# ScalarE's instruction order written out by hand from step 4 of a fused attention and feed-forward kernel

## The chip, the cores and the metric

One core of one Trainium2 chip runs the whole program. The metric is device time in microseconds, the median of several executions. Before the change it is 610.69 us (3 runs, 610.4 to 610.88).

## The reference

Attention with 4 batches, 8 heads, 768 positions and head dimension 64, in fp32. A query sees the first 8 keys and the 96 keys up to its own position, with a bias that grows with the distance. The output, as 3072 tokens by 512, is the input `x` of a gated feed-forward without a nonlinearity:

```
scores = where(keep, q @ k.T / 8 + bias, -1e9)
a = exp(scores - max(scores)); a = a / (sum(a) + 1e-9)
x = (a @ v), heads side by side        # 3072 x 512
out = ((x @ w1) * (x @ w2)) @ w3 @ w_out   # 512 -> 1024 -> 1024 -> 512
```

## The kernel before

**Attention.** The work is cut into 12 chunks of 256 queries (`c`, three to a batch) and 4 pairs of heads; a step `s` does two pairs of one chunk, so there are 24 steps (0 to 23) and a closing visit. In a step TensorE first does the products with the values of the step before (`values`, L457 and L459, into PSUM tile `v`), then the scores of this step (L406, into `s`). ScalarE and VectorE copy `v` out as a high and a low part (`xh`, `xl`, L63 and L64). Then `rows` does for each of 8 blocks (two pairs, two halves `j` of 128 queries, two heads `u`): VectorE adds the bias and takes the maximum (L421), ScalarE takes the exponential in place in `pr` and its sum (L422). `softmax` adds 1e-9 to the sums and inverts them on VectorE (L427, L428) and scales `pr`: the blocks of head `u` = 0 on ScalarE (L434, four a step, called the scalings here), the others on VectorE (L436). `flip` (called through `turn`, four times a step) transposes one half's blocks on TensorE (L445, L447) into the only buffer of `t`, and ScalarE copies it out as `ph` (L449). The first chunk of each batch (`c` = 0, 3, 6, 9) has narrower blocks, 128 columns for 232, in its first half.

**Feed-forward.** `FeedForward.run` is a generator of matmul pieces. For each of 8 blocks `f0` of the hidden dimension, TensorE computes `x @ w1` into a PSUM tile (`m_c_f0_0`, 12 matmuls, L161 to L163), which ScalarE evicts to `a` (L168); then `x @ w2` into the second tile (`m_c_f0_1`), which VectorE multiplies with `a` to `g` (L171); ScalarE and VectorE split `g` to `gh` and `gl` (L63, L64). There are two PSUM buffers for `m`, so `m` of the next block's first half takes the buffer that `a` has read. Then the product with the output weights (`w3 @ w_out`, folded into one matrix in the first steps) goes through tiles `o` (L178 to L180), ScalarE evicts them (L184) and SyncE stores them. From chunk 2 on a run does 512 tokens (two chunks), before that 256 with two blocks `f0` in one tile. The generator yields after 6 matmuls (a half tile), after the eviction, and after the split; `slices(k)` pulls `k` such pieces. A run of 512 tokens takes 48 pieces, the work of four steps: steps 8, 9, 10 and 11 have the run of chunks 2 and 3, and so on. Three of the four steps begin with a first half `m_c_f0_0` (f0 = 0, 3, 6), the fourth with a piece of `o`. Before step 4 there are weights to be prepared as well.

**What sets the order.** TensorE's instructions are in program order (L606). Those of VectorE and SyncE are in program order until the first steps are done, and are placed by the Tile scheduler afterwards (L607 to L620); those of ScalarE are placed by the scheduler throughout. In program order a step is: `visit`, `rows`, `softmax`, `loads` of the next step, then (from step 8 on) `slices(5)`, a `turn`, `slices(2)`, a `turn`, and so on. Each engine takes its own list in order and waits on semaphores of the others.

Of the kernel before, what the change touches and what calls it, by code (L numbers as in the profile page):

```python
# [22 lines left out]
NQ = 2  # L23
# [12 lines left out]
STEP = 2  # L36
# [24 lines left out]
def split(nc, hi, lo, x):  # L61

    nc.scalar.activation(hi, x, AF.Copy)  # L63
    nc.vector.tensor_tensor(out=lo, in0=x, in1=hi.bitcast(F32), op=ALU.subtract)  # L64


class FeedForward:
# [25 lines left out]
    def next(self, ring, slots):  # L93
        self.turn[ring] += 1
        return slots[(self.turn[ring] - 1) % len(slots)]
# [93 lines left out]
@with_exitstack  # L189
def attention_moe(ctx: ExitStack, tc: tile.TileContext, qk, vx, w1, w2, w3t, w_out, ns, out):  # L190
    nc = tc.nc
    cp = ctx.enter_context(tc.tile_pool(name="const", bufs=1))

    ident = cp.tile([P, P], F32, name="ident")
    make_identity(nc, ident)
    nt = cp.tile([P, 4], I32, name="nt")
    nf = cp.tile([P, 4], F32, name="nf")
    ff = FeedForward(ctx, tc, w1, w2, w3t, w_out, out)
    oki = cp.tile([P, 1], I32, name="oki")
    banded(tc, ff, ns, nt, nf, oki, ident, qk, vx)  # L200
    ok = nc.values_load(oki[0:1, 0:1])
    with tc.If(ok == 0):
        dense(tc, ff, nf, ident, qk, vx)
# [121 lines left out]
def banded(ctx, tc, ff, ns, nt, nf, oki, ident, qk, vx):  # L325


    nc = tc.nc
# [51 lines left out]
    def load(c, hp):  # L380
        b, cb = divmod(c, NCB)
        k0 = 0 if cb else BW
        qr = ld.tile([P, QW], F32, tag="qr", name=f"qr_{c}_{hp}")
        nc.sync.dma_start(out=qr[:, k0:], in_=qk[b, cb, hp, :, k0:])
        return qr

    def load_values(c, hp):
        b, cb = divmod(c, NCB)
        nw = 2 * NQ if cb else 2 * NQ - 1
        vr = ld.tile([P, 2 * NQ, 2 * D], F32, tag="vr", bufs=2 * STEP, name=f"vr_{c}_{hp}")  # L390
        nc.sync.dma_start(out=vr[:, :nw], in_=vx[b, cb, hp, :, :nw])
        return vr

    def scores(c, hp, qr):

        ps = sc[hp % STEP]
        for j in range(NQ):
            w0 = BW if c % NCB == 0 and j == 0 else 0  # L400
            for g in range(P // HQ):
                cols = slice(max(w0, g * HQ), BW + (g + 1) * HQ)
                q0 = KW + j * P + g * HQ
                for u in range(2):
                    m = qr[u * D:(u + 1) * D]
                    nc.tensor.matmul(ps[u][g * HQ:(g + 1) * HQ, j, cols], lhsT=m[:, q0:q0 + HQ], rhs=m[:, j * SLOT:][:, cols], start=True, stop=True)  # L406
        return ps

    def rows(c, hp, ps):

        pr = at.tile([P, NQ, 2, UW], F32, tag="pr", name=f"pr_{c}_{hp}")
        mx = at.tile([P, NQ, 2], F32, tag="mx", bufs=3, name=f"mx_{c}_{hp}")
        sm = at.tile([P, NQ, 2], F32, tag="sm", bufs=3, name=f"sm_{c}_{hp}")
        for j in range(NQ):
            first = c % NCB == 0 and j == 0
            w0 = BW if first else 0
            for u in range(2):
                h = 2 * hp + u
                bias = bias0[:, h, :] if first else biasw[:, h, :]
                m = mx[:, j, u:u + 1]  # L420
                nc.vector.tensor_tensor_reduce(out=pr[:, j, u, w0:], in0=ps[u][:, j, w0:UW], in1=bias, scale=-SCALE, scalar=3.0e38, op0=ALU.add, op1=ALU.min, accum_out=m)  # L421
                nc.scalar.activation(pr[:, j, u, w0:], pr[:, j, u, w0:], AF.Exp, bias=m, scale=-1.0, accum_out=sm[:, j, u:u + 1])  # L422
        return pr, sm

    def softmax(c, hp, pr, sm, scaled):

        nc.vector.tensor_scalar(out=sm, in0=sm, scalar1=1e-9, scalar2=None, op0=ALU.add)  # L427
        nc.vector.reciprocal(out=sm, in_=sm)  # L428
        for j in range(NQ):
            w0 = BW if c % NCB == 0 and j == 0 else 0  # L430
            for u in range(2):
                x, r = pr[:, j, u, w0:], sm[:, j, u:u + 1]
                if u == 0 or scaled is nc.scalar:
                    nc.scalar.activation(x, x, AF.Copy, scale=r)  # L434
                else:
                    nc.vector.tensor_scalar(out=x, in0=x, scalar1=r, scalar2=None, op0=ALU.mult)  # L436
        return pr

    def flip(c, hp, j, pr):

        first = c % NCB == 0 and j == 0
        nk = 1 if first else 2
        pt = ps_t.tile([P, 2, 2, P], F32, tag="t", name=f"t_{c}_{hp}_{j}")
        for u in range(2):
            nc.tensor.transpose(pt[:, u, 0], pr[:, j, u, BW:UW], ident)  # L445
            if not first:
                nc.tensor.transpose(pt[:, u, 1], pr[:, j, u, 0:P], ident)  # L447
        ph = at.tile([P, 2, 2, P], F32, tag="ph", bufs=4, name=f"ph_{c}_{hp}_{j}")
        nc.scalar.activation(ph[:, :, :nk], pt[:, :, :nk], AF.Copy)  # L449
        return ph  # L450

    def values(uu, c, hp, vr, phs):
        for j, ph in enumerate(phs):
            first = c % NCB == 0 and j == 0
            for u in range(2):
                rows, o = slice(u * D, (u + 1) * D), uu[u * D:(u + 1) * D, j * P:(j + 1) * P]
                nc.tensor.matmul(o, lhsT=vr[:, j, rows], rhs=ph[:, u, 0], start=True, stop=first)  # L457
                if not first:
                    nc.tensor.matmul(o, lhsT=vr[:BW, 2 * NQ - 1 - j, rows], rhs=ph[:BW, u, 1], start=False, stop=True)  # L459
# [3 lines left out]
    n = NC * NP // STEP  # L463
    pairs = lambda s: [divmod(STEP * s + i, NP) for i in range(STEP)]
# [3 lines left out]
    def slices(k):  # L468
        while k > 0 and work:
            if next(work[0], "end") == "end":  # L470
                work.pop(0)
            else:
                k -= 1

    def loads(s, keys=True, vals=True):
        if s < n and keys:
            qrs[s] = [load(*p) for p in pairs(s)]
        if s < n and vals:
            vrs[s] = [load_values(*p) for p in pairs(s)]

    def visit(s):
        if s:
            c, h0 = pairs(s - 1)[0]
            if h0 == 0 and c % 2 == 0:
                xs[c // 2] = [xp.tile([P, NCC, W], F32R, tag=tag, name=f"{tag}_{c}") for tag in ("xh", "xl")]
            uu = ps_v.tile([P, STEP, T], F32, tag="v", name=f"v_{c}_{h0}")
            for i, p in enumerate(pairs(s - 1)):
                values(uu[:, i], *p, vrs[s - 1][i], phs[s - 1][NQ * i:NQ * (i + 1)])
        ps = [scores(*p, t) for p, t in zip(pairs(s), qrs[s])] if s < n else []
        if s:  # L490
            x2 = xs[c // 2]
            xc = [x[:, :, c % 2 * T:][:, :, :T] for x in x2]
            split(nc, *(x[:, h0:h0 + STEP] for x in xc), uu)
            if h0 + STEP == NP and c < 2:
                work.append(ff.run(c, *xc, c * T, T))
            elif h0 + STEP == NP and c % 2:
                work.append(ff.run(c, *x2, (c - 1) * T, W))
        return ps

    def all_rows(s, ps):  # L500
        return [rows(*p, x) for p, x in zip(pairs(s), ps)]

    def turn(s, m, prs):
        phs.setdefault(s, []).append(flip(*pairs(s)[m // NQ], m % NQ, prs[m // NQ][0]))
# [100 lines left out]
    SLICES = [()] * 3 + [(4, 2, 2, 1, 1)] * 3 + [(4, 2, 1, 1, 1)] * 2 + [(5, 2, 2, 2, 1)] * (n - 8)  # L605
    with tc.manual_schedule(engines={mybir.EngineType.PE}):  # L606
        with tc.manual_schedule(engines={mybir.EngineType.DVE, mybir.EngineType.SP}):  # L607
            first_steps()
        for s in range(4, n + 1):
            rs = all_rows(s, visit(s))  # L610
            for p, r in zip(pairs(s), rs):
                softmax(*p, *r, nc.vector)
            if s == n:
                break
            loads(s + 1)
            for m in range(STEP * NQ):
                slices(SLICES[s][m])
                turn(s, m, rs)
            slices(SLICES[s][-1])
        slices(10 ** 6)  # L620


def lay_out(q, k, v, n_global, n_local, moe_w1, moe_w2, moe_w3, moe_w_out):
# [42 lines left out]
```

## Time and profile before

| | before |
|---|---|
| median of 3 runs | 610.69 us (610.4 to 610.88) |
| the profiled execution, its own time | 609.55 us |
| its span | 607.8 us |
| TensorE matmul busy, of the span | 578.6 us, 95% |
| ScalarE busy | 287.6 us, 47% |
| VectorE busy | 261.3 us, 43% |
| DMA, mean over the span | 89 GB/s |

How to read the rows of the views: a row of the timeline has the start in us from the span's start, the duration, the engine (PE is TensorE, ACT is ScalarE, DVE is VectorE), the line of the kernel, the operation, the tile written and the tiles read with buffer numbers left out, the shape, a count where equal instructions in a row were merged, and in brackets the idle time of the engine before it with what ended it. A row of the waits has the engine and line that waited, the one that ended the wait, the total in us, how many times, and the longest. The end of a matmul is modelled; its start is recorded.

### The profile page before, as it was taken

What the parts mean: (1) busy time and instruction counts of PE and PEld (TensorE: products, weight loads), DVE (VectorE), ACT (ScalarE), POOL (GpSimd) and SP (SyncE); (2) the same over time, 40 slices, a digit from 0 to 9 for tenths busy, and PEclk for the clock granted to TensorE, in tenths of its full rate; (3) what the DMA queues carried; (4) which work ended last, traced back from release to release, by engine and by line L of the source; (5) the groups of instructions that cost most, each with busy time, mean ns of one, the idle gap of its engine ahead of it and who ended that gap; (6) DMA issues with size and microseconds to landing.
All of it is one profiled execution on the core that took longest, in us unless ns stands there. A gap on an engine that the chain in (4) does not pass through costs nothing.

```text
span 607.8 us, 9908 instructions
## 1 busy us (share of the span) xinstructions
PE 578.6 (95%) x3872; PEld 455.5 (75%) x3872; DVE 261.3 (43%) x851; ACT 287.6 (47%) x777; POOL 1.3 (0%) x10
## 2 busy tenths in 40 slices
PE   2998998999999999999999999999999999999995
PEld 0444568989977787887787887787878778888884
DVE  8999998432334424304442322542342451212200
ACT  3065677654455635525544544653553653522210
POOL 0000000000000000000000000000000000000000
PEclk9999999999999999999999999999999999999999
DMA  8897653222023202211220330120331120000001
GB/s 305 304 340 253 212 208 116 79 80 78 27 71 95 78 2 77 79 65 50 78 70 8 113 113 1 61 63 1 125 100 34 44 78 18 36 17 1 0 27 48
DMA packets 23240, 54.01 MB, mean 89 GB/s; under 512 B 2704, under 2 KB 4752, under 8 KB 23184
## 3 DMA queue, kind: packets, MB, share of 16 engines
q1 hardware_dynamic: 23184, 53.29, 25.7%
q8 instruction: 32, 0.52, 0.4%
q14 instruction: 24, 0.20, 0.1%
HBM read 46.99 MB, written 6.29 MB: 88 GB/s over the span
## 4 chain that ended last, share of the span: by engine, by line
PE 70%; ACT 13%; DVE 12%; issue 2%; DMA 2%; SPq 0%; DVEq 0%; ACTq 0%
PE m L161 11%; PE m L163 11%; PE m L162 10%; PE o L178 7%; PE o L180 7%; PE o L179 7%; ACT pr L422 7%; PE v L457 3%; PE t L445 3%; PE t L447 3%; ACT pr L434 3%; PE v L459 3%; PE w L142 2%; PE s L406 2%; DVE t L56 1%
## 5 line engine op out<-in xcount | busy, mean ns | idle before, releaser
L422 ACT ACTIVATE pr<-pr,mx 128x232 f32<-128x232 f32 (+1 forms) x192 | 88.4, 462 | 47.7 <-DVE mx L421 47.7
L449 ACT ACTIVATE ph<-t 128x512 f32<-128x512 f32 (+1 forms) x96 | 53.9, 561 | 101.5 <-PE t L447 93.1
L171 DVE TENSOR_TENSOR g<-m,a 128x512 f32<-128x512 f32 x48 | 33.2, 691 | 142.7 <-PE m L163 131.1
L161 PE MATMUL m<-xh,w1h 128*128 128x512 f32 (+1 forms) x224 | 85.8, 383 | 6.8 <-ACT a L168 6.8
L161 PE MATMUL m<-xh,w2h 128*128 128x512 f32 (+1 forms) x224 | 82.9, 370 | 0.3 <-ACT a L168 0.3
L163 PE MATMUL m<-xh,w1l 128*128 128x512 f32 (+1 forms) x224 | 80.8, 361 | 0.0
L162 PE MATMUL m<-xl,w1h 128*128 128x512 f32 (+1 forms) x224 | 80.7, 360 | 0.0
L163 PE MATMUL m<-xh,w2l 128*128 128x512 f32 (+1 forms) x224 | 80.7, 360 | 0.0
L162 PE MATMUL m<-xl,w2h 128*128 128x512 f32 (+1 forms) x224 | 80.5, 359 | 0.0
L178 PE MATMUL o<-wh,gh 128*128 128x512 f32 x192 | 78.2, 407 | 0.0
L180 PE MATMUL o<-wh,gl 128*128 128x512 f32 x192 | 75.3, 392 | 0.0
L179 PE MATMUL o<-wl,gh 128*128 128x512 f32 x192 | 75.0, 390 | 0.0
L142 PE MATMUL w<-wo,t 128*128 128x512 f32 x128 | 61.0, 622 | 12.1 <-DVE wo L58 11.2
L64 DVE TENSOR_TENSOR xl<-v,xh 128x512 fp32r<-128x512 f32 x24 | 16.6, 690 | 121.0 <-ACT xh L63 120.9
L63 ACT ACTIVATE gh<-g 128x512 fp32r<-128x512 f32 x48 | 30.2, 630 | 64.6 <-DVE g L171 64.6
L161 PEld LDWEIGHTS m<-xh,w1h 128*128 128x128 f32 x224 | 42.2, 189 | 20.0 <-ACT a L168 11.9
L142 PEld LDWEIGHTS w<-wo,t 128*128 128x128 f32 x128 | 24.1, 198 | 40.0 <-issue 22.4
L421 DVE CUSTOM_DVE_ANT_0 pr<-s,biasw 128x232 f32<-128x232 f32 x160 | 53.4, 394 | 0.0
L445 PE MATMUL t<-ident,pr 128*128 128x128 f32 x192 | 45.8, 273 | 3.7 <-ACT pr L434 3.4
L64 DVE TENSOR_TENSOR gl<-g,gh 128x512 fp32r<-128x512 f32 x48 | 33.2, 692 | 34.4 <-ACT gh L63 34.4
L161 PEld LDWEIGHTS m<-xh,w2h 128*128 128x128 f32 x224 | 42.3, 189 | 6.8 <-issue 0.7
L163 PEld LDWEIGHTS m<-xh,w1l 128*128 128x128 f32 x224 | 42.2, 189 | 6.7
(84 smaller groups left out, 816.1 us busy)
## 6 DMA issues: line engine op xcount, KB each, us to landing
qr<-qk SPq DMA_DIRECT2D x32, 312.0 KB, 3.8
vr<-vx SPq DMA_DIRECT2D x32, 256.0 KB, 3.0
stage<-w3t SPq DMA_DIRECT2D x15, 512.0 KB, 6.4
out_dram<-ot SPq DMA_DIRECT2D x24, 256.0 KB, 2.0
raws<-w SPq DMA_DIRECT2D x10, 512.0 KB, 5.7
qr<-qk SPq DMA_DIRECT2D x16, 260.0 KB, 3.4
vr<-vx SPq DMA_DIRECT2D x16, 192.0 KB, 2.7
stage<-w SPq DMA_DIRECT2D x6, 512.0 KB, 7.2
```

Source lines behind the costliest of these rows:

```text
L64: nc.vector.tensor_tensor(out=lo, in0=x, in1=hi.bitcast(F32), op=ALU.subtract)
L142: nc.tensor.matmul(ps, lhsT=self.t3[f, z][:, i * P:(i + 1) * P].bitcast(F32), rhs=self.wo[:, k].bitcast(F32), start=k == 0, stop=k == NFC - 1)
L161: nc.tensor.matmul(ps[:, z], lhsT=mh, rhs=xh[:, i], start=i == 0, stop=False)
L162: nc.tensor.matmul(ps[:, z], lhsT=mh, rhs=xl[:, i], start=False, stop=False)
L163: nc.tensor.matmul(ps[:, z], lhsT=ml, rhs=xh[:, i], start=False, stop=i == NCC - 1)
L178: nc.tensor.matmul(ps, lhsT=gh[:, f, ts], rhs=self.wh[:, f], start=f == 0, stop=False)
L179: nc.tensor.matmul(ps, lhsT=gh[:, f, ts], rhs=self.wl[:, f], start=False, stop=False)
L180: nc.tensor.matmul(ps, lhsT=gl[:, f, ts], rhs=self.wh[:, f], start=False, stop=f == NFC - 1)
L421: nc.vector.tensor_tensor_reduce(out=pr[:, j, u, w0:], in0=ps[u][:, j, w0:UW], in1=bias, scale=-SCALE, scalar=3.0e38, op0=ALU.add, op1=ALU ...
L422: nc.scalar.activation(pr[:, j, u, w0:], pr[:, j, u, w0:], AF.Exp, bias=m, scale=-1.0, accum_out=sm[:, j, u:u + 1])
L445: nc.tensor.transpose(pt[:, u, 0], pr[:, j, u, BW:UW], ident)
L449: nc.scalar.activation(ph[:, :, :nk], pt[:, :, :nk], AF.Copy)
```

## The change

ScalarE's list is in program order too from step 4 on (a `manual_schedule` for Activation around the loop), and the program order of a step is written differently: two pieces of the feed-forward are pulled between `rows` and `softmax`, and that many fewer before the first `turn`. The second piece ends where the eviction `a` of the first half is issued, so that in the steps that begin with a first half, `a` stands between the eight exponentials and the four scalings.

```
-        for s in range(4, n + 1):
-            rs = all_rows(s, visit(s))
-            for p, r in zip(pairs(s), rs):
-                softmax(*p, *r, nc.vector)
-            if s == n:
-                break
-            loads(s + 1)
-            for m in range(STEP * NQ):
-                slices(SLICES[s][m])
-                turn(s, m, rs)
-            slices(SLICES[s][-1])
-        slices(10 ** 6)
+        with tc.manual_schedule(engines={mybir.EngineType.Activation}):
+            for s in range(4, n + 1):
+                rs = all_rows(s, visit(s))
+                if s == n:
+                    break
+
+                slices(2)
+                for p, r in zip(pairs(s), rs):
+                    softmax(*p, *r, nc.vector)
+                loads(s + 1)
+                slices(SLICES[s][0] - 2)
+                for m in range(STEP * NQ):
+                    turn(s, m, rs)
+                    slices(SLICES[s][m + 1])
+            slices(10 ** 6)
```

On TensorE, SyncE and GpSimd the lists are the same instructions in the same order as before. VectorE's differs in step 7 alone: there `g` (L171) moves ahead of one L427, and a `gl` (L64) ahead of one L436. ScalarE's list moves in three ways. In the names below, `pr_4_0` is chunk 4, pair 0; `a_3_0` and `m_3_0_0` are the run that ends with chunk 3, block 0; `ph_2_3_0` is chunk 2, pair 3, half 0; the last number is a running number of the tile and differs between the two programs.

First, in the twelve steps 8 to 10, 12 to 14, 16 to 18 and 20 to 22. ScalarE in step 8, before:

```order
L422 ACTIVATE pr_4_0_1868,sm_4_0_1870<-pr_4_0_1868,mx_4_0_1869 128x232 x4
L422 ACTIVATE pr_4_1_1879,sm_4_1_1881<-pr_4_1_1879,mx_4_1_1880 128x232 x4
L434 ACTIVATE pr_4_0_1868<-pr_4_0_1868,sm_4_0_1870 128x232 x2
L434 ACTIVATE pr_4_1_1879<-pr_4_1_1879,sm_4_1_1881 128x232 x2
L168 ACTIVATE a_3_0_1925<-m_3_0_0_1912 128x512
L63 ACTIVATE gh_3_1910<-g_3_0_1940 128x512
L449 ACTIVATE ph_4_0_0_1956<-t_4_0_0_1951 128x512
```

These are the rows of ScalarE at the same place of step 8 with the change:

```order
L422 ACTIVATE pr_4_0_1870,sm_4_0_1872<-pr_4_0_1870,mx_4_0_1871 128x232 x4
L422 ACTIVATE pr_4_1_1881,sm_4_1_1883<-pr_4_1_1881,mx_4_1_1882 128x232 x4
L168 ACTIVATE a_3_0_1907<-m_3_0_0_1894 128x512
L434 ACTIVATE pr_4_0_1870<-pr_4_0_1870,sm_4_0_1872 128x232 x2
L434 ACTIVATE pr_4_1_1881<-pr_4_1_1881,sm_4_1_1883 128x232 x2
L63 ACTIVATE gh_3_1892<-g_3_0_1942 128x512
L449 ACTIVATE ph_4_0_0_1958<-t_4_0_0_1953 128x512
```

The eviction `a` moved ahead of the four scalings; nothing else moved.

Second, in steps 4, 5 and 6 one copy `ph` and the split `gh` next to it change places. ScalarE in step 5 (the run of 256 tokens of chunk 1), before:

```order
L168 ACTIVATE a_1_0_1363<-m_1_0_0_1338 128x512
L449 ACTIVATE ph_2_2_1_1370<-t_2_2_1_1365 128x512
L449 ACTIVATE ph_2_3_0_1406<-t_2_3_0_1401 128x512
L63 ACTIVATE gh_1_1336<-g_1_0_1397 128x512
L449 ACTIVATE ph_2_3_1_1426<-t_2_3_1_1421 128x512
```

These are ScalarE's rows at the same place of step 5 with the change:

```order
L168 ACTIVATE a_1_0_1365<-m_1_0_0_1340 128x512
L449 ACTIVATE ph_2_2_1_1372<-t_2_2_1_1367 128x512
L63 ACTIVATE gh_1_1338<-g_1_0_1399 128x512
L449 ACTIVATE ph_2_3_0_1408<-t_2_3_0_1403 128x512
L449 ACTIVATE ph_2_3_1_1428<-t_2_3_1_1423 128x512
```

The split of `g` now stands ahead of the copy of the third transposition. In steps 4 and 6 it stands ahead of the copy of the second one (`ph_2_0_1`, `ph_3_0_1`).

Third, in steps 4, 6 and 7 a split `gh` moves ahead of all four scalings (in step 4 it stood between the second and the third). ScalarE in step 7, before:

```order
L422 ACTIVATE pr_3_3_1710,sm_3_3_1712<-pr_3_3_1710,mx_3_3_1711 128x232 x2
L434 ACTIVATE pr_3_2_1699<-pr_3_2_1699,sm_3_2_1701 128x128
L434 ACTIVATE pr_3_2_1699<-pr_3_2_1699,sm_3_2_1701 128x232
L434 ACTIVATE pr_3_3_1710<-pr_3_3_1710,sm_3_3_1712 128x128
L434 ACTIVATE pr_3_3_1710<-pr_3_3_1710,sm_3_3_1712 128x232
L63 ACTIVATE gh_1_1336<-g_1_6_1753 128x512
L449 ACTIVATE ph_3_2_0_1779<-t_3_2_0_1776 128x2x128
```

These are ScalarE's rows at the same place of step 7 with the change:

```order
L422 ACTIVATE pr_3_3_1712,sm_3_3_1714<-pr_3_3_1712,mx_3_3_1713 128x232 x2
L63 ACTIVATE gh_1_1338<-g_1_6_1735 128x512
L434 ACTIVATE pr_3_2_1701<-pr_3_2_1701,sm_3_2_1703 128x128
L434 ACTIVATE pr_3_2_1701<-pr_3_2_1701,sm_3_2_1703 128x232
L434 ACTIVATE pr_3_3_1712<-pr_3_3_1712,sm_3_3_1714 128x128
L434 ACTIVATE pr_3_3_1712<-pr_3_3_1712,sm_3_3_1714 128x232
L449 ACTIVATE ph_3_2_0_1781<-t_3_2_0_1778 128x2x128
```

`gh` moved from behind the scalings to ahead of them.

## Prediction

> **What bounds the kernel now.** The page comes first: who is busy.
>
> ```profile
> span 607.8 us, 9908 instructions
> PE 578.6 (95%) x3872; PEld 455.5 (75%) x3872; DVE 261.3 (43%) x851; ACT 287.6 (47%) x777; POOL 1.3 (0%) x10
> ```
>
> TensorE is the only engine near its span, so a microsecond that it doesn't wait is a microsecond gained, and ScalarE and VectorE matter where they make it wait. So the second view is the waits of TensorE, cut to steps 8 to 23 (183 to 537 us), then to steps 12 and 13 and to step 18:
>
> ```profile
> PE m L161 <- ACT a L168: 6.8, 12, 0.7
> ```
>
> ```profile
> PE m L161 <- ACT a L168: 0.4, 2, 0.2
> ```
>
> ```profile
> PE m L161 <- ACT a L168: 0.2, 1, 0.2
> ```
>
> In 354 us TensorE waits for one thing alone, twelve times: for ScalarE's eviction `a`. Three of the twelve waits are short (those steps work on the narrower blocks), nine are long. The third view is the timeline at the first of them, in step 8: TensorE, then ScalarE, then VectorE.
>
> ```profile
> 186.45 0.39 PE L163 MATMUL m<-xh,w1l 128*128 128x512 f32 x1
> ...
> 188.94 0.39 PE L162 MATMUL m<-xl,w2h 128*128 128x512 f32 x1
> 189.17 0.39 PE L163 MATMUL m<-xh,w2l 128*128 128x512 f32 x1
> 190.30 0.50 PE L161 MATMUL m<-xh,w1h 128*128 128x512 f32 x1 [0.74 <-ACT a L168]
> 190.63 0.39 PE L162 MATMUL m<-xl,w1h 128*128 128x512 f32 x1
> ...
> 191.79 0.27 PE L445 MATMUL t<-ident,pr 128*128 128x128 f32 x1
> ```
>
> ```profile
> 187.68 0.47 ACT L422 ACTIVATE pr<-pr,mx 128x232 f32<-128x232 f32 x1
> ...
> 188.16 1.61 ACT L434 ACTIVATE pr<-pr,sm 128x232 f32<-128x232 f32 x4
> 189.68 0.57 ACT L168 ACTIVATE a<-m 128x512 f32<-128x512 f32 x1
> ```
>
> ```profile
> 188.70 0.59 DVE L436 TENSOR_SCALAR pr<-pr,sm 128x232 f32<-128x232 f32 x2
> 190.28 0.69 DVE L171 TENSOR_TENSOR g<-m,a 128x512 f32<-128x512 f32 x1 [0.99 <-ACT a L168]
> ```
>
> Block 0's first half, which `a` reads, is complete at 186.45 + 0.39 = 186.84. ScalarE is in its exponentials until 188.15, then does four scalings, and starts `a` at 189.68, which ends at 190.25. TensorE has started the last matmul of the second half at 189.17 and wants the buffer for block 1; it gets it at 190.30.
>
> **What a stall costs.** By starts, not by the bracket. Matmuls start 189.17 − 188.94 = 0.23 us apart, so block 1 would have begun at 189.40; it begins 0.90 later. The matmul behind it follows after 0.33, where 0.23 is the pace: 0.10 more. A long stall costs 1.00. A short one, in step 12:
>
> ```profile
> 278.89 0.39 PE L163 MATMUL m<-xh,w2l 128*128 128x512 f32 x1
> 279.47 0.50 PE L161 MATMUL m<-xh,w1h 128*128 128x512 f32 x1 [0.19 <-ACT a L168]
> ```
>
> 0.58 − 0.23 = 0.35, and the same 0.10 (my estimate from the long one): 0.45. A check from outside: 30 matmuls stand between the scores and the first transposition of a step, with the stall in step 8 (start below, end at 191.79 above), without one in step 11, whose pieces are of `o`:
>
> ```profile
> 183.82 0.50 PE L161 MATMUL m<-xh,w1h 128*128 128x512 f32 x1
> ```
>
> ```profile
> 251.96 0.50 PE L178 MATMUL o<-wh,gh 128*128 128x512 f32 x1
> ...
> 258.89 0.27 PE L445 MATMUL t<-ident,pr 128*128 128x128 f32 x1
> ```
>
> 7.97 against 6.93: 1.04. All twelve are worth 9 x 1.00 + 3 x 0.45 = 10.35 us.
>
> [...] The row says that TensorE sat idle for 0.74 in the first stall, and 6.8 in all. [...] By the row the sum would be 6.8. [...]
>
> **The change in steps 8 to 23.** No instruction is added or removed on ScalarE; twelve evictions move ahead of four scalings each. In step 8 `a` then starts when the exponentials end, at 188.16 (its half tile has been complete for 1.32 us), and ends at 188.73. TensorE wants the buffer at 189.40: 0.67 to spare, and the whole stall goes. In the short kind `a` came 0.55 earlier against TensorE (1.00 − 0.45), so more is to spare.
>
> What is late next? The scalings start by 188.73, and the four take 1.61; they follow each other by (189.68 − 188.16) / 4 = 0.38, so one takes 1.61 − 3 x 0.38 = 0.47. The first is done by 189.20, the fourth by 190.34. The first transposition follows block 1's first half, 191.79 − 190.30 − 0.10 = 1.39 behind its start: at 189.40 + 1.39 = 190.79. It needs the first scaling alone (and VectorE's half, which does not move); even the fourth would be in time. VectorE's `g` no longer waits for `a` but for the second half, complete at 189.17 + 0.39 = 189.56, behind L436, which ends at 189.29. So `g` runs at about 189.6 to 190.3, and `gh` still follows the scalings on ScalarE. Nothing else of a step hangs on ScalarE's clock time: the next step's `xh`, maxima and exponentials start from TensorE's products. With cover gone, the cost would be the wait at the transposition instead. The loads on SyncE and the few instructions of GpSimd keep their places. Cost of these: zero.
>
> **The change in steps 4 to 7.** The swap of `ph` and `gh` adds a wait at the head of ScalarE's list: `ph`, ready, stands behind `gh`, which waits for `g`. TensorE waits for that `ph`, since `t` has one buffer. Steps 5 and 6:
>
> ```profile
> 142.70 0.69 DVE L171 TENSOR_TENSOR g<-m,a 128x512 f32<-128x512 f32 x1 [6.99 <-PE m L163]
> ...
> 143.06 0.60 ACT L449 ACTIVATE ph<-t 128x512 f32<-128x512 f32 x1 [2.65 <-PE t L447]
> ...
> 143.56 0.62 ACT L63 ACTIVATE gh<-g 128x512 fp32r<-128x512 f32 x1
> ...
> 144.30 0.27 PE L445 MATMUL t<-ident,pr 128*128 128x128 f32 x1
> ```
>
> ```profile
> 158.60 0.69 DVE L171 TENSOR_TENSOR g<-m,a 128x512 f32<-128x512 f32 x1 [2.52 <-PE m L163]
> ...
> 160.20 0.38 PE L445 MATMUL t<-ident,pr 128*128 128x128 f32 x2
> ```
>
> In step 5 `gh` can start at 143.42 (`g` ends 143.39) and ends at 144.04; `ph` follows, overlapping by 0.1, and ends at 144.55, where TensorE wants the buffer at 144.30. That is 0.25 to 0.3 late. In step 6 the transpositions want it 1.60 behind the start of `g`, as in step 5 (144.30 − 142.70): the same again. Together I take 0.6, between 0.5 and 0.8 (with a restart of 0.10 each). Step 4 has the same swap:
>
> ```profile
> 120.30 0.69 DVE L171 TENSOR_TENSOR g<-m,a 128x512 f32<-128x512 f32 x1 [3.00 <-PE m L163]
> ...
> 123.23 0.27 PE L445 MATMUL t<-ident,pr 128*128 128x128 f32 x1
> ```
>
> There 2.93 lie between, so `ph`, done 1.85 behind the start of `g` as in step 5 (144.55 − 142.70), is 1.1 early: zero.
>
> `gh` ahead of the scalings needs `g` early and the first transposition late. Step 4, then step 6:
>
> ```profile
> 114.37 0.68 DVE L171 TENSOR_TENSOR g<-m,a 128x512 f32<-128x512 f32 x1
> ...
> 115.19 0.85 ACT L434 ACTIVATE pr<-pr,sm 128x232 f32<-128x232 f32 x2
> ...
> 116.72 0.27 PE L445 MATMUL t<-ident,pr 128*128 128x128 f32 x1
> ```
>
> ```profile
> 152.68 0.68 DVE L171 TENSOR_TENSOR g<-m,a 128x512 f32<-128x512 f32 x1
> ...
> 153.40 1.44 ACT L434 ACTIVATE pr<-pr,sm 128x128 f32<-128x128 f32 x4
> ...
> 155.25 0.38 PE L445 MATMUL t<-ident,pr 128*128 128x128 f32 x2
> ```
>
> In step 4 `g` is done at 115.05, before ScalarE is free at 115.19; `gh` takes 0.62 and the first scaling 0.47 behind it, to 116.28, ahead of 116.72. In step 6 `g` is done at 153.36, ScalarE is free at 153.40, and the first scaling ends by 154.49, ahead of 155.25. Both zero; if the cover were gone, up to 0.6 (one `gh`) each.
>
> In step 7 TensorE waits for this very `gh`, and then for its low part:
>
> ```profile
> 171.84 0.61 ACT L63 ACTIVATE gh<-g 128x512 fp32r<-128x512 f32 x1
> 172.13 0.38 PE L445 MATMUL t<-ident,pr 128*128 128x128 f32 x2
> ...
> 172.51 0.50 PE L178 MATMUL o<-wh,gh 128*128 128x512 f32 x1
> ...
> 172.84 0.40 PE L179 MATMUL o<-wl,gh 128*128 128x512 f32 x1
> 173.24 0.50 PE L180 MATMUL o<-wh,gl 128*128 128x512 f32 x1
> ```
>
> `gh` comes four scalings earlier, over 1 us, if `g` is there (VectorE's list too has it earlier now). Two transpositions take 0.38 where one takes 0.27, so they start 0.11 apart, and L178 could follow the first by 0.22 instead of 0.38. L180 comes 0.40 behind L179 instead of 0.23, and its restart adds 0.10. 0.16 + 0.17 + 0.10 = 0.4 gained; at least zero.
>
> **The sum.** 10.35 + 0.4 − 0.6 = 10.15 us. The profiled execution took 609.55 (1.75 outside the span); it would take 599.4. The median of the runs shown is 1.14 higher, 610.69, so the forecast is 610.69 − 10.15 = 600.5, 1.7% faster.
>
> **The rivals.** *Only the idle time comes back.* TensorE's rows of waits name 6.8 us; if starts behind a wait are recorded late, or part of the bubble belongs to the queue, the gain is 6.8, and steps 4 to 7 cancel: 603.9. For it: the view's own number. Against it: 7.97 and 6.93 are starts of other instructions, and differ by 1.04. Chance 0.09.
>
> *The eviction waits at the head of the list, and the kernel is slower.* Place: `a` behind the exponentials in the twelve steps. If its half tile comes late there, or the exponentials end early, `a` holds the scalings, `gh` and the copies behind it. Before, no scaling stood behind it. Price: held by x, block 1 comes x − 0.67 later than TensorE wants it, and the transpositions with it. Up to 0.67 it is free, at 1.67 the stall of 1.00 is back (610.7), and from there the kernel is slower than before: at 2.0 by 12 x 0.33 = 4 us, 614.7. For it: the change binds the two streams of work into one list, where before the scheduler chose. Against it: `a` is ready 1.32 us before its place, so the half tile would have to come 1.32 + 1.67 = 3 us later than it does, and what sets its time, TensorE, only gets earlier, as do the exponentials with it. Chance 0.05, of which 0.02 end within the measurement. [...]
>
> *Something else holds the buffer.* If the wait put down to `a` ended by chance with it, nothing changes: 610.7. But `a` is the only reader of that half, and the waits name it twelve times of twelve. Chance 0.01.
>
> **How the numbers follow.** The forecast has 0.85. Its own ends: all stalls at the price of the check (9 x 1.04 + 3 x 0.5 = 10.9), the swap free and step 7 in full, 11.3 off, 599.4; without step 7, and 0.8 for the swap, 9.55 off, 601.1. Median and run differ by a few tenths, so the low end is 599.0. The high end takes in the first rival, 603.9 and a tenth: 604.0. A measurement of this kernel can tell about 0.2% (1.2 us) from no change; faster by more has 0.85 + 0.09 = 0.94, within it 0.03, slower 0.03.
>
> **What would show it.** With the change, the waits of TensorE in steps 8 to 23 have no row for L168; 30 matmuls take 6.93 in every step; each of the twelve steps is 1.0 or 0.5 shorter, the rest as long as before; two short waits of `t` for `ph` appear in steps 5 and 6, and L178 and L180 wait no more in step 7. The forecast is wrong if L445 waits for L434 or L436 in those steps, if L161 waits for anything else, or if the steps without a stall change.

## The result, and the profile after

The changed kernel takes 600.01 us (median of 4 runs, 599.5 to 600.6), the kernel before in the same comparison 610.55 (609.41 to 610.88): a ratio of 0.9831, with a 95% interval of 0.9814 to 0.9848. Forecast were 600.5 and a ratio of 0.983. The profiled execution took 599.7 us; the page of the changed kernel, its span, its engines, and its chain that ended last:

```profile
span 597.9 us, 9930 instructions
PE 574.8 (96%) x3872; PEld 456.3 (76%) x3872; DVE 261.2 (44%) x851; ACT 287.3 (48%) x777; POOL 1.3 (0%) x10
...
PE 84%; DVE 10%; DMA 3%; ACT 1%; issue 0%; SPq 0%; DVEq 0%; ACTq 0%
```

The kernel before has this row for its chain:

```profile
PE 70%; ACT 13%; DVE 12%; issue 2%; DMA 2%; SPq 0%; DVEq 0%; ACTq 0%
```

The span is 9.9 us shorter. ScalarE does the same work in as many instructions, and in the chain it has 1%, where the kernel before had 13%: it no longer holds TensorE. The waits of TensorE, cut to steps 8 to 23 as in the prediction (183 to 530 us, a little earlier at the end), have no row at all. The timeline of step 8 shows why: TensorE, ScalarE and VectorE around the place of the first stall.

```profile
189.18 0.39 PE L162 MATMUL m<-xl,w2h 128*128 128x512 f32 x1
189.41 0.39 PE L163 MATMUL m<-xh,w2l 128*128 128x512 f32 x1
189.64 0.39 PE L161 MATMUL m<-xh,w1h 128*128 128x512 f32 x1
189.86 0.39 PE L162 MATMUL m<-xl,w1h 128*128 128x512 f32 x1
...
191.00 0.27 PE L445 MATMUL t<-ident,pr 128*128 128x128 f32 x1
```

```profile
187.91 0.47 ACT L422 ACTIVATE pr<-pr,mx 128x232 f32<-128x232 f32 x1
...
188.39 0.58 ACT L168 ACTIVATE a<-m 128x512 f32<-128x512 f32 x1
188.86 1.62 ACT L434 ACTIVATE pr<-pr,sm 128x232 f32<-128x232 f32 x4
190.63 0.63 ACT L63 ACTIVATE gh<-g 128x512 fp32r<-128x512 f32 x1
```

```profile
188.93 0.59 DVE L436 TENSOR_SCALAR pr<-pr,sm 128x232 f32<-128x232 f32 x2
189.91 0.69 DVE L171 TENSOR_TENSOR g<-m,a 128x512 f32<-128x512 f32 x1 [0.38 <-PE m L163]
```

The eviction `a` ends at 188.97; block 1 begins at 189.64, 0.23 behind the matmul ahead of it, which is the pace. Its cover, the time by which it is done before TensorE needs it, is 189.64 − 188.97 = 0.67 us, to the hundredth what was forecast. The first scaling is done about 0.47 behind 188.86, and the transposition that needs it starts at 191.00: 1.67 us of cover.

Where the 9.9 us came from is read from three starts of TensorE in each kernel: the value products that open step 4, those that open step 8, and the last matmul. Before:

```profile
107.59 0.45 PE L457 MATMUL v<-ph,vr 128*64 128x128 f32 x4
...
181.00 0.71 PE L457 MATMUL v<-ph,vr 128*64 128x128 f32 x8
...
601.24 0.39 PE L180 MATMUL o<-wh,gl 128*128 128x512 f32 x1
```

With the change:

```profile
107.65 0.45 PE L457 MATMUL v<-ph,vr 128*64 128x128 f32 x4
...
181.24 0.71 PE L457 MATMUL v<-ph,vr 128*64 128x128 f32 x8
...
591.28 0.39 PE L180 MATMUL o<-wh,gl 128*128 128x512 f32 x1
```

From step 8 on, 420.24 became 410.04: 10.20 us less. Steps 4 to 7 took 73.41 and take 73.59: 0.18 more.

The same starts, taken at the head of every step, put both differences in their places. The nine steps with a long stall are 0.97 to 1.03 us shorter (8.83 together), the three with a short one 0.44 to 0.48 (1.36 together). The four other steps from step 8 on, and all that follows step 23, are as long as before to the hundredth. Of the early steps, step 4 is unchanged, steps 5 and 6 are 0.37 longer each, and step 7 is 0.56 shorter.

In steps 4 to 7 the swap's two waits are there, as TensorE's weight-load rows in the waits (steps 4 to 7) say:

```profile
PEld t L445 <- ACT ph L449: 0.7, 2, 0.3
```

And step 7 has lost its wait for `gh` and `gl`:

```profile
171.29 0.62 ACT L63 ACTIVATE gh<-g 128x512 fp32r<-128x512 f32 x1
...
172.93 0.38 PE L445 MATMUL t<-ident,pr 128*128 128x128 f32 x2
173.06 0.48 PE L178 MATMUL o<-wh,gh 128*128 128x512 f32 x1
173.38 0.40 PE L179 MATMUL o<-wl,gh 128*128 128x512 f32 x1
173.61 0.39 PE L180 MATMUL o<-wh,gl 128*128 128x512 f32 x1
```

L178 follows the transpositions by 0.13 (before 0.38), L180 follows L179 by 0.23 (before 0.40).

### The profile page after: what moved, and what is told of

Same layout as the page of the kernel before. It is cut to its first block, busy times and chain, and to the rows that moved or that the text cites. A ratio compares the mean times of both kernels' runs of the same rounds, so it can differ in the third digit from the quotient of the medians.

```text
span 597.9 us, 9930 instructions
## 1 busy us (share of the span) xinstructions
PE 574.8 (96%) x3872; PEld 456.3 (76%) x3872; DVE 261.2 (44%) x851; ACT 287.3 (48%) x777; POOL 1.3 (0%) x10
## 4 chain that ended last, share of the span: by engine, by line
PE 84%; DVE 10%; DMA 3%; ACT 1%; issue 0%; SPq 0%; DVEq 0%; ACTq 0%
PE m L161 15%; PE m L163 14%; PE m L162 14%; PE o L178 8%; PE o L180 7%; PE o L179 7%; PE s L406 4%; PE v L457 4%; PE t L445 3%; PE v L459 3%; PE t L447 3%; PE w L142 2%; DVE t L56 1%; DVE t L58 1%; DMA stage<-w3t 1%; DMA raws<-w 1%
## 5 line engine op out<-in xcount | busy, mean ns | idle before, releaser
L171 DVE TENSOR_TENSOR g<-m,a 128x512 f32<-128x512 f32 x48 | 33.2, 691 | 133.4 <-PE m L163 132.7
L161 PE MATMUL m<-xh,w1h 128*128 128x512 f32 (+1 forms) x224 | 84.5, 377 | 0.0
L178 PE MATMUL o<-wh,gh 128*128 128x512 f32 x192 | 78.2, 407 | 0.0
L180 PE MATMUL o<-wh,gl 128*128 128x512 f32 x192 | 75.2, 392 | 0.0
L179 PE MATMUL o<-wl,gh 128*128 128x512 f32 x192 | 75.0, 390 | 0.0
L64 DVE TENSOR_TENSOR xl<-v,xh 128x512 fp32r<-128x512 f32 x24 | 16.6, 690 | 122.5 <-ACT xh L63 122.5
L163 PEld LDWEIGHTS m<-xh,w2l 128*128 128x128 f32 x224 | 42.2, 189 | 6.5
```

Of the source, the lines that this page charges most:

```text
L161: nc.tensor.matmul(ps[:, z], lhsT=mh, rhs=xh[:, i], start=i == 0, stop=False)
L163: nc.tensor.matmul(ps[:, z], lhsT=ml, rhs=xh[:, i], start=False, stop=i == NCC - 1)
L171: nc.vector.tensor_tensor(out=g, in0=ps, in1=a, op=ALU.mult)
L178: nc.tensor.matmul(ps, lhsT=gh[:, f, ts], rhs=self.wh[:, f], start=f == 0, stop=False)
L179: nc.tensor.matmul(ps, lhsT=gh[:, f, ts], rhs=self.wl[:, f], start=False, stop=False)
L180: nc.tensor.matmul(ps, lhsT=gl[:, f, ts], rhs=self.wh[:, f], start=False, stop=f == NFC - 1)
```

## The experiments

The theory to be tested: each stall was TensorE waiting for its second buffer, the eviction has a cover of 0.67 us where it now stands, and only time beyond that cover is lost. Its rivals: the order written by hand is what helps, wherever the eviction stands; every scaling ahead of the eviction has its price; the earlier the better; and a wait at the head of ScalarE's list costs its own length. There are six kernels, four run on one chip and two on another, each against the kernel before on the same chip (610.1 and 610.24 us). In all of them the lists of TensorE and SyncE are those of the kernel before. VectorE's list is placed by the scheduler; in the two kernels whose eviction stands between or ahead of the exponentials, `g` also moves ahead of two L436, in nine and in twelve steps.

**The change once more** (no edit), as the measure for its neighbours.

> The changed kernel once more, as the measure for the three kernels beside it on the same chip. Every theory: ratio to before 0.983, about 600.0 us, and no wait of TensorE for the eviction in steps 8 to 23.

600.39 us, ratio 0.9836 (0.9816 to 0.9856). Its starts:

```profile
182.08 0.71 PE L457 MATMUL v<-ph,vr 128*64 128x128 f32 x8
...
592.13 0.39 PE L180 MATMUL o<-wh,gl 128*128 128x512 f32 x1
```

From step 8 on it took 410.05 us, as in the first profile (410.04).

**The order by hand alone.** The pieces go back behind the softmax.

```
-                if s == n:
-                    break
-
-                slices(2)
                 for p, r in zip(pairs(s), rs):
                     softmax(*p, *r, nc.vector)
+                if s == n:
+                    break
                 loads(s + 1)
-                slices(SLICES[s][0] - 2)
+                slices(SLICES[s][0])
```

> ScalarE's list in program order from step 4 on, as in the change, but the pieces stay where they were, so that the eviction stands behind the scalings again in the twelve steps. Buffer theory: all twelve stalls are back, and of steps 4 to 7 only the swap's two waits of 0.30 stay, since the split is behind the scalings again in step 7: before + 0.6, 611.2, ratio 1.001. Rival, the order written by hand is what helps: 600 to 603, ratio below 0.99.

610.96 us, ratio 1.0009 (1.0001 to 1.0018). TensorE's waits in steps 8 to 23 of this kernel, then its three starts:

```profile
PE m L161 <- ACT a L168: 6.8, 12, 0.7
```

```profile
108.18 0.45 PE L457 MATMUL v<-ph,vr 128*64 128x128 f32 x4
...
182.36 0.71 PE L457 MATMUL v<-ph,vr 128*64 128x128 f32 x8
...
602.60 0.39 PE L180 MATMUL o<-wh,gl 128*128 128x512 f32 x1
```

The row is the one of the kernel before, to the digit, and from step 8 on it takes 420.24, to the hundredth. Steps 4 to 7 take 74.18, 0.77 more than before (0.6 expected): 0.37 in step 5, 0.37 in step 6 and 0.03 in step 7. The order by hand gains nothing by itself; the gain is the eviction's place.

**The eviction behind two scalings** (from step 8 on).

```
-                slices(2)
-                for p, r in zip(pairs(s), rs):
+                if s < 8:
+                    slices(2)
+                for i, (p, r) in enumerate(zip(pairs(s), rs)):
                     softmax(*p, *r, nc.vector)
+                    if i == 0 and s >= 8:
+                        slices(2)
```

> From step 8 on the eviction stands behind the first pair's two scalings and ahead of the second pair's. Buffer theory (TensorE wants the buffer 0.67 us behind the end of the eviction, in the long kind; only what goes beyond that cover is lost): the eviction ends 2 x 0.38 = 0.76 later than in the change, so a wait comes back of 0.76 - 0.67 + 0.05 = 0.14 and a restart of 0.10 in the nine long steps, nothing in the three short ones: 2.2 us longer than the change, 602.2. Rival, each scaling ahead of the eviction costs its time (0.38, so 0.76 in every step): 12 x 0.76 = 9 us longer, 609. Rival, the order written by hand is what helps and the place does not matter: as the change, 600.0.

601.9 us, ratio 0.9871 (0.9848 to 0.9893); the change beside it took 600.39. The intervals overlap, so the times alone leave it open; the trace decides. Step 8 of this kernel, ScalarE, then TensorE from there to the end:

```profile
188.87 0.58 ACT L168 ACTIVATE a<-m 128x512 f32<-128x512 f32 x1
```

```profile
180.96 0.71 PE L457 MATMUL v<-ph,vr 128*64 128x128 f32 x8
...
189.13 0.39 PE L163 MATMUL m<-xh,w2l 128*128 128x512 f32 x1
189.50 0.50 PE L161 MATMUL m<-xh,w1h 128*128 128x512 f32 x1
189.84 0.40 PE L162 MATMUL m<-xl,w1h 128*128 128x512 f32 x1
...
593.05 0.39 PE L180 MATMUL o<-wh,gl 128*128 128x512 f32 x1
```

The eviction ends at 189.45, and TensorE wanted the buffer at 189.13 + 0.23 = 189.36. Block 1 starts 0.05 behind the eviction's end and 0.37 − 0.23 = 0.14 late, and the matmul behind it another 0.34 − 0.23 = 0.11 (this second part is called the restart below): 0.25 in all. In the other eight long steps block 1 is 0.09 late, with the same restart. From step 8 on the kernel takes 412.09, 2.05 more than the change, where 2.2 were expected. All of it is in the nine long steps (0.29 in step 8, 0.21 or 0.22 in the others); the three short ones lose nothing. The waits of steps 8 to 23 list no row for it, since the modelled end of the matmul ahead reaches past 189.50 (189.13 + 0.39 = 189.52): a bubble that the starts show and the idle time does not. The cover is 0.67, and of the 0.76 of two scalings ahead of the eviction only what went beyond it was paid, with the restart.

**The eviction between the exponentials** (from step 8 on), earlier than in the change.

```
-                rs = all_rows(s, visit(s))
+                rs = []
+                for i, (p, x) in enumerate(zip(pairs(s), visit(s))):
+                    if i and 8 <= s < n:
+                        slices(2)
+                    rs.append(rows(*p, x))
...
-                slices(2)
+                if s < 8:
+                    slices(2)
```

> From step 8 on the eviction stands between the two pairs' exponentials, still earlier than in the change. There it has to wait at the head of ScalarE's list for its half tile, about 0.6 us in the long kind (complete 186.84, first pair's exponentials done 186.26), and holds the second pair's exponentials, the scalings and all behind them by that. Buffer theory: the first scaling then ends at 189.7, the first transposition wants it at 190.8, so the wait of ScalarE costs nothing and an earlier eviction gains nothing: as the change, 600.0, within 0.5. Rival, earlier is better (each us that the eviction comes earlier is worth something): 2 to 5 us shorter. Rival, a wait at the head of the list costs its length: 12 x 0.6 = 7 us longer, 607.

599.24 us, ratio 0.9822 (0.9803 to 0.9841); the change 600.39. Step 8 of this kernel, ScalarE, then TensorE from there to the end:

```profile
187.09 0.60 ACT L168 ACTIVATE a<-m 128x512 f32<-128x512 f32 x1 [0.52 <-PE m L163]
187.59 0.48 ACT L422 ACTIVATE pr<-pr,mx 128x232 f32<-128x232 f32 x1
```

```profile
181.22 0.71 PE L457 MATMUL v<-ph,vr 128*64 128x128 f32 x8
...
591.26 0.39 PE L180 MATMUL o<-wh,gl 128*128 128x512 f32 x1
```

The eviction waits 0.52 us at the head of the list for its half tile, with four exponentials and all else behind it, and comes 1.3 us earlier than in the change. Neither matters: from step 8 on, 410.04 again, and each of these steps is as long as with the change to the hundredth. Earlier is not better here, and this wait of ScalarE, 0.52 in step 8, cost nothing, since TensorE did not yet need what stands behind it.

**The eviction ahead of all exponentials** (from step 8 on). This makes the wait at the head of the list real that the prediction's slower rival speaks of, by an earlier place and not, as there, by a half tile that comes late.

```
-                rs = all_rows(s, visit(s))
+                ps = visit(s)
+                if 8 <= s < n:
+                    slices(2)
+                rs = all_rows(s, ps)
...
-                slices(2)
+                if s < 8:
+                    slices(2)
```

> From step 8 on the eviction stands ahead of all eight exponentials, which is the rival of the prediction that ends slower, made real: it waits at the head of ScalarE's list for its half tile (complete 186.84) while the first exponential was to start at 184.36, and holds the exponentials and scalings by some 3.0 us. Buffer theory: exponentials 187.4 to 191.2, first scaling done 191.65, and the first transposition, wanted at 190.79, waits 0.9 in the nine long steps and 0.4 in the three short ones: 9 x 0.9 + 3 x 0.4 = 9.3 us longer than the change, 609.3, about as slow as before, with TensorE's waits now at the transposition for the scaling, none at the buffer. Rival, a wait at the head of the list costs its length: 12 x 2.5 = 30 us longer. Rival, earlier is better: 600 or less.

610.97 us, ratio 1.0009 (1.0 to 1.0017): the whole gain is lost. TensorE's waits in steps 8 to 23 of this kernel, then ScalarE in step 8, then TensorE from there to the end:

```profile
PE t L445 <- ACT pr L434: 8.3, 12, 0.8
```

```profile
187.32 0.60 ACT L168 ACTIVATE a<-m 128x512 f32<-128x512 f32 x1 [3.66 <-PE m L163]
187.81 0.48 ACT L422 ACTIVATE pr<-pr,mx 128x232 f32<-128x232 f32 x1
...
191.59 1.61 ACT L434 ACTIVATE pr<-pr,sm 128x232 f32<-128x232 f32 x4
```

```profile
181.44 0.71 PE L457 MATMUL v<-ph,vr 128*64 128x128 f32 x8
...
189.61 0.39 PE L163 MATMUL m<-xh,w2l 128*128 128x512 f32 x1
189.84 0.39 PE L161 MATMUL m<-xh,w1h 128*128 128x512 f32 x1
...
190.97 0.39 PE L163 MATMUL m<-xh,w1l 128*128 128x512 f32 x1
192.12 0.33 PE L445 MATMUL t<-ident,pr 128*128 128x128 f32 x1 [0.76 <-ACT pr L434]
...
602.36 0.39 PE L180 MATMUL o<-wh,gl 128*128 128x512 f32 x1
```

There is no wait for the buffer (189.61 to 189.84 is the pace), and twelve at the transposition, which starts 1.15 behind the matmul ahead of it instead of 0.23. From step 8 on it takes 420.92: 10.88 more than the change, where 9.3 were expected; the exponentials ended 0.4 later than worked out (`a` started at 187.32, and each exponential behind it follows by 0.47). Counted from the start of step 8, the last exponential comes 3.0 us later than with the change and the first scaling 2.5. Only what goes beyond the cover at the transposition is lost: 0.97 to 1.04 us in a long step, 0.53 to 0.63 in a short one.

**The copies ahead of the split again** (steps 4 to 6). `g` and its split are kept back until the `turn` behind them has been issued; `flush` issues what was kept, and is also called ahead of every further piece and between the two early pieces and the softmax. `product` holds the three lines that are taken out.

```
-            g = mp.tile([P, nf, width], F32, tag="g", name=f"g_{c}_{f0}")
-            nc.vector.tensor_tensor(out=g, in0=ps, in1=a, op=ALU.mult)
-            split(nc, gh[:, fs], gl[:, fs], g)
+            def product(ps=ps, a=a, fs=fs, f0=f0):
...
+            if self.hold:
+                self.kept.append(product)
+            else:
+                product()
...
+                ff.hold = s < 8
...
                     turn(s, m, rs)
+                    flush()
```

> The change with the copies of the transpositions put back ahead of the split in steps 4, 5 and 6, as they stood before; the split stays ahead of the scalings in steps 4, 6 and 7. Theory of the swap: the two waits of the transpositions for the copy, 0.30 each in steps 5 and 6, go, and nothing replaces them: 0.6 us shorter than the change, 599.4, which the times can hardly tell and the starts of TensorE can. Rival, the split comes late for the low part instead: the 0.6 returns as a wait of a product for gh or gl: 600.0.

599.23 us, ratio 0.9822 (0.9804 to 0.9841), against 600.39 of the change; the times can't tell the two apart. The starts can. Its value products of steps 4 and 8, and its last matmul (line numbers have moved by 6):

```profile
107.54 0.45 PE L463 MATMUL v<-ph,vr 128*64 128x128 f32 x4
...
180.38 0.71 PE L463 MATMUL v<-ph,vr 128*64 128x128 f32 x8
...
590.43 0.39 PE L186 MATMUL o<-wh,gl 128*128 128x512 f32 x1
```

Steps 4 to 7 take 72.84, 0.75 less than with the change and 0.57 less than before; the rest takes 410.05. The swap cost 0.37 in each of steps 5 and 6 (0.3 of waiting, and most of the rest is the restart behind it), the split ahead of the scalings in step 7 (with `g`, which moved on VectorE there) gains 0.56, and this kernel has both right. By the trace it is the best of the seven.

## Why the prediction was right

- *The price of a stall by starts* held. Twelve stalls were put at 10.35 us; from step 8 on, 10.20 were saved. The nine long ones gave 8.83 for 9.00, since the stall of step 8, from which the price was read, is the longest; the three short ones gave 1.36 for 1.35. The first rival, that only the idle time of 6.8 us comes back, is out. The view of the waits under-stated these bubbles: in `order_only` it says 6.8 again where the starts say 10.20, and in the kernel with two scalings ahead it says nothing where they say 2.05.
- *The cover* of 0.67 us was read off one timeline, and two experiments agree with it: a place 0.76 later makes block 1 of step 8 0.14 late and costs a restart, and a place 1.3 us earlier gains nothing.
- *What is late next* held: nothing. The first transposition was put 1.59 us behind the first scaling's end and had 1.67. When the scalings come 2.5 us late it is the next wait, as the last experiment but one shows.
- *Steps 4 to 7* were put at +0.6 for the swap and −0.4 for step 7, +0.2 in all; +0.18 was measured. The net agrees by luck, since both parts were put too low by much the same: the swap cost 0.37 + 0.37 = 0.74, and step 7 gave 0.56. In step 7 the sum let L178 follow the first transposition by 0.22; it follows by 0.13. The swap's wait itself was 0.3 a step, as put; a restart behind each was allowed for in the upper end of that term, 0.8, and not in its middle.
- *The slower rival* did not come about, and its mechanism is real: with the eviction ahead of all exponentials ScalarE sits idle for 3.66 us in step 8 until the half tile is there, and the first exponential starts only behind the eviction, at 187.81. Its price, block 1 later by the hold less 0.67, was for an eviction whose half tile comes late, and no run has that. With the eviction ahead of the exponentials the eviction itself is early; the scalings behind it are late, and the exponentials' delay of 3.0 us loses 0.97 in step 8, at the transposition.

So the main term was right by its mechanism, and each of the three terms was measured apart. From step 4 on, 10.02 us were saved of 10.15 forecast. That the median, 600.01, lies within 0.5 of the forecast is no finer a test: the four runs lie between 599.5 and 600.6.

## What to carry to other kernels

On an engine that is not the bound, order its list by who on the bounding engine waits next, and read each instruction's cover from one timeline: its end, against the start at which its consumer would come at the pace. In this kernel moving an instruction within its cover was free in either direction (the eviction 1.3 us earlier than in the change, the scalings 0.46 later than before: 410.04 us from step 8 on, either way); beyond it, the excess was paid once per repetition, at the consumer whose cover ran out first (in step 8, 0.25 at the buffer with two scalings ahead, 0.97 at the transposition with the eviction ahead of the exponentials). Price a matmul bubble by starts against the pace, plus the restart, and not by the idle time that a waits view names (here 10.20 against 6.8).

## What the runs showed of the hardware that was not expected

**A bubble cost a restart.** In these runs the first matmul behind a bubble (a gap between the starts on TensorE beyond the pace) held up the second by 0.10 to 0.11 us (0.33 to 0.34 us from start to start, where 0.23 is the pace), be the bubble 0.90 us long (before, step 8), 0.35 (before, step 12) or 0.14 (two scalings ahead, step 8). At a transposition it was less, 0.05 to 0.06 (0.16 to 0.17 for 0.11). In the kernel with two scalings ahead, whose stalls are short, this is about half of the price: 0.11 of 0.25 in step 8. Why the restart is there, no run shows.

**From step 4 on the schedule repeated to the hundredth.** From step 8 on, the change took 410.04 and 410.05 us in its two profiled executions (steps 4 to 7: 73.59 and 73.58), on runs whose spans were 597.9 and 598.6. Step 4 of the second began at

```profile
108.50 0.45 PE L457 MATMUL v<-ph,vr 128*64 128x128 f32 x4
```

against 107.65 in the first: the two differ by 0.85 there, and by 0.85 still at the last matmul. What varies ahead of step 4 stays open, and whether the other executions differ there too no trace shows. So a change of half a microsecond in the steady part, which the times of this kernel can't tell, is plain in one trace by starts, as the 0.75 of `ph_first` was.
